# A two-layer decode block on one core: w_o kept by heads, one unit instead of two in small products at a layer's end, and layer 2's rolled block one unit later

## The chip, the cores and the metric

The kernel runs on one core of a Trainium2 chip. The metric is the device time of one execution in microseconds. Three runs of the kernel before took 650.52, 650.72 and 650.79 us; the median is 650.72 us.

A core has five engines with instruction streams of their own: TensorE (PE in the profile; its weight loads are shown apart as PEld), VectorE (DVE), ScalarE (ACT), GpSimd (POOL) and SyncE (SP). SP issues the transfers, and 16 DMA engines carry them out. The engines wait for each other on semaphores. The matmuls write to eight banks of an accumulator memory (`ps`).

## The reference

Four sequences decode one token each, through attention, FFN, attention, FFN, with the same weights twice. Only the shapes matter here:

```python
B, Sq, D = 4, 1, 512
Hq, Hkv, Sk, Dh = 32, 8, 8192, 128
F = 1792
# attention: x + A(layernorm(x))
q = (x @ wq)                       # 32 heads of 128; 4 heads share one key/value head
scores = einsum("bhqd,bhkd->bhqk", q, k) * Dh ** -0.5
o = einsum("bhqk,bhkd->bhqd", softmax(scores), v)
return o.reshape(B, Sq, Hq * Dh) @ wo
# FFN: x + B(layernorm(x))
return (silu(x @ w_gate) * (x @ w_up)) @ w_down
```

All inputs are bf16. The key and value caches have 2 MB for each of the 32 pairs of a sequence and a key/value head. They are read once per layer, except for what the second layer still finds on the chip.

## The kernel before, in words

**Units.** A unit is one pair of a sequence b and a key/value head g, u = 4 g + b. Layer 1 takes the units 0 to 31. Layer 2 starts with 29, 30 and 31, whose K and V are still on the chip (`NRES = 3`), and then takes 0 to 28 (`unit_order`, line 310). Each unit needs 2 MB of K and 2 MB of V. Eight slots of 2 MB hold them; `home` (line 336) says which slot.

**One unit.** K arrives with 64 positions per partition. DVE transposes it in eight pieces (`turn`), PE multiplies each piece with the placed query (`scores`, four products of 256 columns per piece). Then come the softmax steps: the row maximum (`max_p`, `max_t`), the exponent on ACT (`exps`), a transpose of the probabilities on DVE (`turn_p`), and the sum and its reciprocal (`total`). The values are multiplied in `values` (line 551) in one of two ways:

- wide: 16 products whose moving operand has 512 columns of V. The result holds every combination of a position group and a slice of V, of which only a part is wanted. ACT copies the first slice with a factor (`own_first`), DVE adds three more (`own_others`), and a product with `head` sums the rows (`add_rows`). All of this goes through one buffer, `acc`. `scale_o` then writes the scaled result to `oT`.
- small: 64 products of 4 columns with V as the weights (`block_last`). The result is the output itself, and only `scale_o` follows.

`NLAST` (line 181) says how many of a layer's last units take the small way. Their V is worked in eight blocks; a layer's last V is loaded in four parts (`split`), so that its blocks can start before all of it is there.

**Output projection.** After the fourth unit of a head group, `out_proj` (line 631) multiplies `oT` with the 512 rows of w_o that belong to it. w_o lies on the chip with 4 KB per partition and group, that is four consecutive rows of w_o. So the rows in `oT` are first reordered: 16 products with columns of the identity matrix (`pick`), a cast on DVE into `o4`, then 16 products with `wo_sb`, then an addition to `xT`. The cast is what waits for w_o's arrival.

**Order.** Nothing is scheduled at run time. Python lists write the order down: `blocks` holds PE's larger pieces, each with a length in us; `advance` counts these lengths down against two lists of follow-up steps, `line` (the softmax of the next unit) and `after` (the sums and scaling of the one before). `flush` empties them where a buffer is needed again. In `block_last`, `flush(after)` stands before the seventh of eight blocks. The instructions of PE, DVE and ACT are recorded on tapes first. `roll` (line 740) finds, for each layer, a stretch that repeats with period four (`CYCLE`), and writes it as a loop with register arithmetic; what is left before and after it is written out. Each engine's loop has its own start and number of turns.

**Transfers.** SP issues all of them in one order (`items`, `pump`): w_q, x, then K and V in the order of use, with a quarter of w_o after each of the positions 3, 6, 9 and 12. A load goes out when its slot is free. At a layer's end w_gate, w_up and w_down follow into slots 6 and 7 and a strip behind them. When the FFN's products are through, the loads of the next units go there. `runs` (line 345) views the source as at least 32 rows of at most 32 KB, so that one transfer has few and long packets.

**Instruction code.** Engines fetch their instructions by DMA as well; the profile shows them as a queue of their own.

Of the kernel before, what the change touches and what calls it, by code (L numbers as in the profile page):

```python
# [8 lines left out]
BF16 = mybir.dt.bfloat16  # L9
U8 = mybir.dt.uint8  # L10
# [135 lines left out]
def bass_interleave_layers__gqa_block_cached__swiglu_ffn__decode_kernel(  # L146
# [12 lines left out]
    B, _, D = A_x.shape  # L159
    _, G, S, Dh = A_k_cache.shape  # L160
    HqDh = A_wq.shape[1]
    Hq = HqDh // Dh
    F = B_w_gate.shape[1]
    REP = Hq // G
    P = 128
# [3 lines left out]
    XB = KT * B  # L169
# [3 lines left out]
    QB = 32  # L173
# [4 lines left out]
    assert XQ <= SW  # L178
    ZP = QB - REP
    NQ = 4  # L180
    NLAST = 2
    NSLOT = 8
    NKEEP = 6
    NV = NB // 2
    RUN = 1 << 15
# [5 lines left out]
    with ExitStack() as es:  # L191
        sb = lambda name, shape, dt: es.enter_context(nc.sbuf_tensor(name, shape, dt))
# [20 lines left out]
        WD = ((0, 6), (6, 12), (12, 14))  # L213
        wq_sb = sb("wq_sb", [P, KT, HqDh], BF16)

        wo_sb = sb("wo_sb", [P, G, REP, D], BF16)
        wo_b = wo_sb[:].rearrange("p g e n -> p (g e n)").bitcast(U8)
        identf = sb("identf", [P, P], FP32)

        ident = identf[:].bitcast(BF16).rearrange("p (x e) -> p x e", e=2)[:, :, 1]  # L220
# [2 lines left out]
        quad = sb("quad", [P, NA], BF16)  # L223
        head = sb("head", [P, REP], FP32)
        rstd = sb("rstd", [P, B], FP32)
        o4 = sb("o4", [P, REP, B], BF16)
        oT = sb("oT", [P, 2, REP, B], BF16)

        acc = sb("acc", [P, Dh], FP32)
# [5 lines left out]
        pb = sb("pb", [P, SW], BF16)  # L235
# [3 lines left out]
        rl = sb("rl", [P, 4, REP], FP32)  # L239
# [4 lines left out]
        n = 2 * FO * B  # L244
# [7 lines left out]
        def bank(k):  # L252
            return ps[:, k * BANKF:(k + 1) * BANKF]

        def bank_bf(k):
# [4 lines left out]
        STEP, TOT, OUTB, LNB = 4, 5, 6, 7  # L260
# [8 lines left out]
        sem_w = {n: [sem(f"sem_{n}{i}") for i in range(c)]  # L269
                 for n, c in (("wq", KT), ("wo", 4), ("wg", 1), ("wu", 2), ("wd", 3))}  # L270
# [32 lines left out]
        rl_of = {}  # L303
# [38 lines left out]
                return 0 if i == NU - 1 else (7, 2, 3, 6)[i % CYCLE]  # L342
            return {NU - 3: 1, NU - 2: 4, NU - 1: 5}.get(i, (5, 0, 4, 1)[i % CYCLE])

        def runs(src):

            n = src.shape[0] * src.shape[1] * 2
            return src.rearrange("(r k) n -> r (k n)", r=32 * -(-n // (32 * RUN)))

        def load_weight(name, i=0):  # L350
            if name == "wq":
                T.dma("sp", [(wq_sb[:, i, :], runs(A_wq[i * P:(i + 1) * P, :]))], sem_w["wq"][i], writes=[f"wq{i}"])
            elif name == "wo":
                n = G // 4
                w = REP * Dh
                T.dma("sp", [(wo_sb[:, g, :, :].rearrange("p e n -> p (e n)"), runs(A_wo[g * w:(g + 1) * w, :]))
                             for g in range(i * n, (i + 1) * n)], sem_w["wo"][i], writes=[f"wo{i}"])
            elif name == "wg":
                T.dma("sp", [(wg_sb[:, k, :], runs(B_w_gate[k * P:(k + 1) * P, :])) for k in range(KT)], sem_w["wg"][0],
                      writes=places + ["wg"])  # L360
            elif name == "wu":
                up = [(wu_sb[k], runs(B_w_up[k * P:(k + 1) * P, :])) for k in range(KT)]
                if i == 0:
                    T.dma("sp", up[:FR], sem_w["wu"][0], writes=["wu"])
                T.dma("sp", up[FR:], sem_w["wu"][1], writes=["wu3"])
            else:

                for j, (a, b) in enumerate(WD):
                    T.dma("sp", [(wd_sb[:, f:f + 2, :].rearrange("p e n -> p (e n)"),
                                  runs(B_w_down[f * P:(f + 2) * P, :])) for f in range(a, b, 2)], sem_w["wd"][j],  # L370
                          writes=[f"wd{j}"])
# [179 lines left out]
        def values(L, u):  # L551
            g, b = unit_gb(u)
            bk = OBK[turn_of[u]]
            def begin():
                flush(line, u)
                flush(after, turn_of[u])

            def end():
                finished(("V", L, u))
                after.extend(rest)  # L560

            def block(i):

                if i == 0:
                    begin()
                s = slot_of["V", L, u]
                v = kv[:, s, :].rearrange("p (q t d) -> p t q d", t=TB, d=Dh)
                for t in range(TB):
                    j = t % NA
                    c0 = t * QB + i * NV * REP  # L570
                    T.pe(bank(bk)[j * QB:j * QB + NV * REP, :], pT[:, turn_of[u], c0:c0 + NV * REP],
                         v[:, t, NV * i:NV * (i + 1), :],
                         reads=[f"s{s}.{NV * i + k}" for k in range(NV)] + [f"pT{turn_of[u]}"], writes=[f"pb{bk}"],
                         sig=(t == TB - 1), start=(i == 0 and t == j), stop=(i == 1 and t >= TB - NA))
                if i == 1:
                    end()

            def own_first():
                T.op("act", lambda e: e.activation(acc[:], bank(bk)[:, 0:Dh], ACTF.Copy, scale=own[:, 0:1]),
                     reads=[f"pb{bk}", "own"], writes=["acc"])  # L580

            def own_others():
                for k in range(1, NV):
                    T.op("dve", lambda e: e.scalar_tensor_tensor(acc[:], bank(bk)[:, k * Dh:(k + 1) * Dh], own[:, k:k + 1],
                                                                 acc[:], op0=ALU.mult, op1=ALU.add),
                         reads=[f"pb{bk}", "own", "acc"], writes=["acc"])

            def add_rows():
                T.pe(bank(LNB)[:, 0:REP], acc[:], head[:], reads=["acc", "head"], writes=[f"pb{LNB}"],
                     start=True, stop=True)  # L590
                scale_o(LNB)

            def block_last(q):

                if q == 0:
                    begin()
                if q == NB - 2:
                    flush(after)
                s = slot_of["V", L, u]
                for t in range(q * TB, (q + 1) * TB):  # L600
                    c0 = (t % TB) * QB + REP * q
                    T.pe(bank(bk)[:, 0:REP], kv[:, s, t * Dh:(t + 1) * Dh], pT[:, turn_of[u], c0:c0 + REP],
                         reads=[f"s{s}.{q}", f"pT{turn_of[u]}"], writes=[f"pb{bk}"], sig=(t % TB == TB - 1),
                         start=(t == 0), stop=(t == TT - 1))
                if q == NB - 1:
                    end()

            def scale_o(k):
                T.op("dve", lambda e: e.tensor_tensor(oT[:, g // (G - 1), :, b], bank(k)[:, 0:REP], rl[:, rl_of[u], :],
                                                      ALU.mult),  # L610
                     reads=[f"pb{k}", f"rl{rl_of[u]}"], writes=[f"oT{g // (G - 1)}"])

            if u in unit_order[L][-NLAST:]:
                rest = [[0.3, turn_of[u], lambda: scale_o(bk)]]
                blocks.extend((0.25, lambda q=q: block_last(q)) for q in range(NB))
            else:
                rest = [[0.1, None, own_first], [0.6, turn_of[u], own_others], [1.3, None, add_rows]]
                blocks.extend((0.5, lambda i=i: block(i)) for i in range(2))
            done.add((L, u))
            if all((L, g * B + k) in done for k in range(B)):  # L620
                rest.append([0.5, None, lambda: out_proj(g)])


# [4 lines left out]
        def wo_at(n):  # L628
            return lambda g: wo_b[:, bass.ds(g * (REP * D * 2) + n * 2, P * 2)].bitcast(BF16)

        def out_proj(g):

            pick = ident.rearrange("p (j e) -> p e j", e=REP)
            ob = bank(OUTB)[:, XB:2 * XB].rearrange("p (e b) -> p e b", b=B)
            for c in range(REP):
                for h in range(REP):
                    T.pe(ob[h * QB:(h + 1) * QB, c, :], pick[:, c, :], oT[:, g // (G - 1), h, :],
                         reads=[f"oT{g // (G - 1)}", "ident"], writes=[f"pb{OUTB}"], sig=(h == REP - 1),
                         start=True, stop=True)
            T.op("dve", lambda e: e.tensor_copy(o4[:], ob),  # L640
                 reads=[f"pb{OUTB}"] + [f"wo{i}" for i in range(4)], writes=["o4"])
            for nt in range(KT):
                for c in range(REP):
                    T.pe(bank(OUTB)[:, nt * B:(nt + 1) * B], ((c, nt), wo_at(c * D + nt * P)), o4[:, c, :], at=g,
                         reads=["o4"], writes=[f"pb{OUTB}"], sig=(c == REP - 1), start=(c == 0), stop=(c == REP - 1))
            add_to_x()


# [91 lines left out]
        def roll(name):  # L740
# [18 lines left out]
            for L in range(2):  # L759
                run = {}  # L760
                for n in range(L * NU + 1, L * NU + NU - CYCLE - 1):
# [2 lines left out]
                            strides(m) == strides(n + (m - n) % CYCLE):  # L764
                        m += 1
                    run[n] = m - n
                n = max(run, key=run.get)
                turns = run[n] // CYCLE + 1
                assert turns >= 3
                step = {}  # L770
# [87 lines left out]
```

## Time and profile before

| | |
|---|---|
| median of 3 runs | 650.72 us |
| the profiled execution's own time | 651.29 us |
| its span, first to last instruction | 649.3 us |
| PE busy | 505.3 us (78%), 4896 products |
| DVE busy | 446.2 us (69%) |
| ACT busy | 116.3 us (18%) |
| DMA, mean over the span | 422 GB/s, 274.27 MB |
| chain that ended last | DMA 50%, DVE 24%, PE 21% |
| w_o's transfers | 8 of 512 KB, 37.7 us to landing (median) |
| pick products, `ps<-oT,identf` | 256, 6.6 us busy in all |
| w_o products, `ps<-o,wo_sb` | 256, 26.5 us busy in all |
| casts, `o<-ps` | 16, 2.3 us busy in all |
| small value products, `ps<-pT,kvf` | 256, 7.8 us busy in all |

How to read it. "Busy" is the time in which at least one instruction of that engine ran. PE's products are pipelined, so that the sum of their durations is more than the busy time. Almost all instructions stand on two lines of the program, L99 for PE and L117 for DVE and ACT, because two helpers record them; one goes by the names of what is written and read. `kvf` is the memory of the eight slots and the FFN's weights, `pb` and `pT` the probabilities before and after the transpose, `acc` the buffer of the sums, `ps` the accumulator banks, `scr` scratch space. "idle before <- X" names what ended a wait; "issue" stands for time in which the engine waited for no semaphore that the profile shows. In the strips of 40 slices each slice is 16.2 us.

### The profile page before, as it was taken

What the parts mean: (1) busy time and instruction counts of PE and PEld (TensorE: products, weight loads), DVE (VectorE), ACT (ScalarE), POOL (GpSimd) and SP (SyncE); (2) the same over time, 40 slices, a digit from 0 to 9 for tenths busy, and PEclk for the clock granted to TensorE, in tenths of its full rate; (3) what the DMA queues carried; (4) which work ended last, traced back from release to release, by engine and by line L of the source; (5) the groups of instructions that cost most, each with busy time, mean ns of one, the idle gap of its engine ahead of it and who ended that gap; (6) DMA issues with size and microseconds to landing.
All of it is one profiled execution on the core that took longest, in us unless ns stands there. A gap on an engine that the chain in (4) does not pass through costs nothing.

```text
span 649.3 us, 12407 instructions
## 1 busy us (share of the span) xinstructions
PE 505.3 (78%) x4896; PEld 324.7 (50%) x4896; DVE 446.2 (69%) x1079; ACT 116.3 (18%) x391; POOL 19.3 (3%) x73
## 2 busy tenths in 40 slices
PE   1657788878868787886877986898888787886886
PEld 1534454545435454553556654555555454553556
DVE  2556676776866767776762386979797777686683
ACT  0021111211211212221220211213131221121120
POOL 0000000000000000000000000000000000000000
PEclk9998787797987879789795978979897969799795
DMA  8999999999999999999999999999999999999996
GB/s 347 427 431 428 433 429 434 428 440 428 432 436 424 444 426 432 439 424 442 428 416 361 421 408 430 417 439 430 432 438 424 438 430 436 436 424 438 430 415 279
DMA packets 13085, 274.27 MB, mean 422 GB/s; under 512 B 2712, under 2 KB 2720, under 8 KB 3744
## 3 DMA queue, kind: packets, MB, share of 16 engines
q1 hardware_dynamic: 13056, 273.89, 98.7%
q8 instruction: 17, 0.28, 0.2%
q14 instruction: 12, 0.10, 0.0%
HBM read 273.88 MB, written 0.00 MB: 422 GB/s over the span
## 4 chain that ended last, share of the span: by engine, by line
DMA 50%; DVE 24%; PE 21%; issue 3%; SPq 1%; ACT 1%; DVEq 0%; POOL 0%; ACTq 0%; POOLq 0%
DMA kvf<-in_A_k_cache_dram 47%; PE ps L99 21%; DVE kvf L117 15%; DVE acc L117 4%; DMA kvf<-in_B_w_up_dram 3%; DVE one L117 1%; DVE pT L117 1%; SPq L135 1%; DVE m L117 1%; DVE scr L117 1%; ACT pb L117 0%; ACT acc L117 0%; DVE oT L117 0%; DVEq L782 0%; SPq L133 0%
## 5 line engine op out<-in xcount | busy, mean ns | idle before, releaser
L117 DVE STREAM_TRANSPOSE kvf<-kvf 128x512 f32<-128x512 f32 x488 | 322.3, 686 | 68.6 <-DMA kvf<-in_A_k_cache_dram 68.6
L99 PE MATMUL ps<-kvf,zq 128*128 128x256 bf16 x2048 | 332.6, 305 | 21.7 <-DVE kvf L117 16.4
L99 PEld LDWEIGHTS ps<-kvf,zq 128*128 128x128 bf16 x2048 | 202.6, 111 | 92.7 <-DVE kvf L117 40.2
L117 ACT ACTIVATE pb<-m 1x128 f32<-1x128 f32 x64 | 19.7, 308 | 441.1 <-DVE m L117 441.1
L99 PE MATMUL ps<-kvf,pT 128*16 128x512 bf16 x960 | 68.0, 407 | 1.4 <-DVE rl L117 1.4
L117 DVE SCALAR_TENSOR_TENSOR acc<-ps,own,acc 128x128 f32<-128x128 f32 x180 | 63.2, 351 | 6.5 <-ACT acc L117 1.9
L99 PE MATMUL ps<-identf,one 128*1 128x128 f32 x64 | 17.9, 279 | 43.2 <-DVE one L117 43.2
L117 DVE TENSOR_REDUCE one<-ps 128x1 f32<-128x256 f32 x64 | 25.9, 405 | 37.0 <-PE ps L99 36.5
L99 PEld LDWEIGHTS ps<-identf,one 128*1 128x1 f32 x64 | 5.1, 80 | 73.6 <-DVE one L117 67.5
L99 PE MATMUL ps<-head,acc 128*128 128x4 f32 x120 | 24.5, 275 | 21.4 <-DVE acc L117 21.3
L99 PEld LDWEIGHTS ps<-head,acc 128*128 128x128 f32 x120 | 20.5, 214 | 37.0 <-DVE acc L117 36.7
L117 ACT ACTIVATE pb<-ps,one,rstd 128x256 bf16<-128x256 f32 x64 | 36.1, 563 | 2.1
L467 POOL TENSOR_TENSOR zq<-scr,quad 128x64 bf16<-128x64 bf16 x62 | 18.1, 293 | 604.0 <-PE ps L99 564.9
L99 PEld LDWEIGHTS ps<-kvf,pT 128*16 128x16 bf16 x960 | 19.1, 91 | 33.8 <-issue 21.9
L99 PE MATMUL ps<-one,pb 1*128 1x1 f32 x128 | 26.2, 272 | 11.5 <-ACT pb L117 11.2
L99 PEld LDWEIGHTS ps<-one,pb 1*128 1x128 f32 x128 | 20.8, 202 | 28.8 <-ACT pb L117 26.0
L99 PE MATMUL ps<-o,wo_sb 128*128 128x4 bf16 x256 | 26.5, 166 | 9.1 <-DVE o L117 9.1
L117 DVE STREAM_TRANSPOSE pT<-pb 128x256 bf16<-128x256 bf16 x64 | 26.1, 408 | 9.7 <-ACT pb L117 9.7
L99 PEld LDWEIGHTS ps<-rsm,one 128*128 128x128 f32 x128 | 23.9, 232 | 12.2 <-ACT rsm L117 10.4
L99 PEld LDWEIGHTS ps<-o,wo_sb 128*128 (+1 forms) x256 | 22.8, 103 | 12.8 <-issue 9.0
L99 PE MATMUL ps<-rsm,one 128*128 128x4 f32 x128 | 21.7, 240 | 9.0 <-ACT rsm L117 9.0
L117 DVE TENSOR_TENSOR xT<-xT,ps 128x16 f32<-128x16 f32 x21 | 3.6, 172 | 33.1 <-PE ps L99 33.1
(61 smaller groups left out, 197.1 us busy)
## 6 DMA issues: line engine op xcount, KB each, us to landing
kvf<-in_A_k_cache_dram SPq DMA_DIRECT2D x60, 2048.0 KB, 28.8
kvf<-in_A_v_cache_dram SPq DMA_DIRECT2D x58, 2048.0 KB, 31.2
wq_sb<-in_A_wq_dram SPq DMA_DIRECT2D x4, 1024.0 KB, 8.4
wo_sb<-in_A_wo_dram SPq DMA_DIRECT2D x8, 512.0 KB, 37.7
kvf<-in_A_v_cache_dram SPq DMA_DIRECT2D x8, 512.0 KB, 14.7
kvf<-in_B_w_gate_dram SPq DMA_DIRECT2D x8, 448.0 KB, 16.8
kvf<-in_B_w_down_dram SPq DMA_DIRECT2D x14, 256.0 KB, 17.6
kvf<-in_B_w_up_dram SPq DMA_DIRECT2D x5, 448.0 KB, 18.0
```

The source lines that it names most:

```text
L99: return e.matmul(out, lhsT=lhsT if at is None else lhsT(place(at)), rhs=rhs, **kw)
L117: self.tape[engname].append((repr((name, args, kw)), lambda e, _: getattr(e, name)(*args, **kw), left, sig, None))
L135: ins = e.add_instruction(mybir.InstDMACopy(name=self.nc.get_next_instruction_name(), mode="Copy", queue="qSPDynamicHW", ins=e.lower_ap_dm ...
L467: T.op(eng, lambda e: e.tensor_tensor(dst, q4, m4_, ALU.mult), reads=keys_ + ["quad"], writes=["zq"])
```

## The change

- `wo_sb` has one row of 1 KB per partition and head: partition p of head h holds row 128 h + p of w_o. It is loaded with 32 transfers of 128 KB (eight per quarter) instead of eight of 512 KB (two per quarter). Each transfer has 16 source rows of 8 KB.
- `out_proj` takes `oT` as it is. The pick products, the cast and `o4` are gone. The wait for w_o's four quarters stands at `scale_o` of a group's last unit.
- `NLAST` is 1. The unit before a layer's last (30 in layer 1, 27 in layer 2) has its values in 16 wide products, with the sums through `acc`.
- `roll` takes, among the starts with the same number of turns, the last one. In layer 2 PE's and ACT's loops begin a unit later (the 6th unit of the layer in the kernel before, the 7th after); in layer 1 the starts are as they were. The number of turns stays 7 and 6 for PE and ACT, and 6 and 6 for DVE.

```diff
-    NLAST = 2
+    NLAST = 1
...
-        wo_sb = sb("wo_sb", [P, G, REP, D], BF16)
-        wo_b = wo_sb[:].rearrange("p g e n -> p (g e n)").bitcast(U8)
+        wo_sb = sb("wo_sb", [P, Hq, D], BF16)
+        wo_b = wo_sb[:].rearrange("p h n -> p (h n)").bitcast(U8)
...
-        o4 = sb("o4", [P, REP, B], BF16)
...
-        def runs(src):
+        def runs(src, least=32):
 
             n = src.shape[0] * src.shape[1] * 2
-            return src.rearrange("(r k) n -> r (k n)", r=32 * -(-n // (32 * RUN)))
+            return src.rearrange("(r k) n -> r (k n)", r=least * -(-n // (least * RUN)))
...
-                n = G // 4
-                w = REP * Dh
-                T.dma("sp", [(wo_sb[:, g, :, :].rearrange("p e n -> p (e n)"), runs(A_wo[g * w:(g + 1) * w, :]))
-                             for g in range(i * n, (i + 1) * n)], sem_w["wo"][i], writes=[f"wo{i}"])
+                n = Hq // 4
+                T.dma("sp", [(wo_sb[:, h, :], runs(A_wo[h * Dh:(h + 1) * Dh, :], 16)) for h in range(i * n, (i + 1) * n)],
+                      sem_w["wo"][i], writes=[f"wo{i}"])
...
+            done.add((L, u))
+            whole = all((L, g * B + k) in done for k in range(B))
...
-                     reads=[f"pb{k}", f"rl{rl_of[u]}"], writes=[f"oT{g // (G - 1)}"])
+                     reads=[f"pb{k}", f"rl{rl_of[u]}"] + [f"wo{i}" for i in range(4) if whole],
+                     writes=[f"oT{g // (G - 1)}"])
...
-            done.add((L, u))
-            if all((L, g * B + k) in done for k in range(B)):
+            if whole:
                 rest.append([0.5, None, lambda: out_proj(g)])
...
         def out_proj(g):
-
-            pick = ident.rearrange("p (j e) -> p e j", e=REP)
-            ob = bank(OUTB)[:, XB:2 * XB].rearrange("p (e b) -> p e b", b=B)
-            for c in range(REP):
-                for h in range(REP):
-                    T.pe(ob[h * QB:(h + 1) * QB, c, :], pick[:, c, :], oT[:, g // (G - 1), h, :],
-                         reads=[f"oT{g // (G - 1)}", "ident"], writes=[f"pb{OUTB}"], sig=(h == REP - 1),
-                         start=True, stop=True)
-            T.op("dve", lambda e: e.tensor_copy(o4[:], ob),
-                 reads=[f"pb{OUTB}"] + [f"wo{i}" for i in range(4)], writes=["o4"])
+            k = g // (G - 1)
             for nt in range(KT):
                 for c in range(REP):
-                    T.pe(bank(OUTB)[:, nt * B:(nt + 1) * B], ((c, nt), wo_at(c * D + nt * P)), o4[:, c, :], at=g,
-                         reads=["o4"], writes=[f"pb{OUTB}"], sig=(c == REP - 1), start=(c == 0), stop=(c == REP - 1))
+                    T.pe(bank(OUTB)[:, nt * B:(nt + 1) * B], ((c, nt), wo_at(c * D + nt * P)), oT[:, k, c, :], at=g,
+                         reads=[f"oT{k}"], writes=[f"pb{OUTB}"], sig=(c == REP - 1), start=(c == 0), stop=(c == REP - 1))
             add_to_x()
...
-                n = max(run, key=run.get)
+                n = max(run, key=lambda n: (run[n] // CYCLE, n))
```

## The prediction

> **What bounds the kernel now.** I read the page's slices first, then busy time by stretch, then the chain of waits around the layers' ends, then the order of time in the last 20 us.
>
> ```profile
> DMA  8999999999999999999999999999999999999996
> GB/s 347 427 431 428 433 429 434 428 440 428 432 436 424 444 426 432 439 424 442 428 416 361 421 408 430 417 439 430 432 438 424 438 430 436 436 424 438 430 415 279
> ...
> q8 instruction: 17, 0.28, 0.2%
> ```
>
> ```profile
> core 0: us, PE busy (x) PEld busy (x) DVE busy (x) ACT busy (x) POOL busy (x), PEclk, DMA share, GB/s
> 80.00:300.00 220.00, 177.13 (x1431) 109.35 (x1431) 158.47 (x371) 39.45 (x134) 6.73 (x23) 0.84 1.00 433
> ...
> 27.00:68.00 41.00, 28.00 (x269) 18.18 (x267) 26.83 (x60) 6.83 (x23) 1.17 (x4) 0.84 1.00 427
> ...
> 344.00:346.00 2.00, 1.26 (x48) 1.29 (x49) 1.14 (x5) 0.25 (x1) 0.00 (x0) 0.50 1.02 414
> 346.00:349.00 3.00, 1.32 (x44) 1.15 (x41) 0.21 (x1) 0.00 (x0) 0.00 (x0) 0.50 0.49 197
> ...
> 386.00:510.00 124.00, 103.68 (x912) 64.23 (x911) 102.73 (x242) 26.00 (x88) 4.39 (x15) 0.92 1.00 430
> ```
>
> The DMA engines are full from 2 to 346 us and again to 643 us: 274 MB at 433 GB/s. No compute in those stretches costs anything. Time can be won or lost in three ways: more DMA time per byte; the hole at 346-349 us, where 197 GB/s instead of 433 means (433 - 197)/433 x 3 = 1.6 us without data; and the tail, once the last weights are there.
>
> The hole, by the chain of waits:
>
> ```profile
> 326.13 18.47 DMA kvf<-in_B_w_up_dram
> 344.61 0.14 issue
> 344.74 1.50 PE ps L99 x51
> 346.24 1.38 issue
> 347.62 0.31 PE ps L99 x5
> 347.92 0.02 issue
> ```
>
> w_up lands at 344.6, PE does 51 of the 56 up products, stands 1.38 us for "issue" (no semaphore, no data), does the last 5, and at 347.99 SP issues the next K, because slot 6 holds w_gate and w_up until then.
>
> The tail, PE in order of time:
>
> ```profile
> 644.10 1.27 PE L99 MATMUL ps<-scr,kvf 128*128 128x4 bf16 x35 [0.43 <-DVE scr L117]
> 645.69 0.70 PE L99 MATMUL ps<-scr,kvf 128*128 128x4 bf16 x21 [0.32 <-issue]
> 646.72 0.59 PE L99 MATMUL ps<-identf,xn 128*4 128x128 bf16 x4 [0.33 <-DVE xn L117]
> ```
>
> From 631 us on the end hangs on a serial chain of small operations (attention, w_o, layer norm, FFN), with another 0.32 us of "issue".
>
> **The change, part by part.**
>
> *w_o on the DMA engines.* 4.19 MB come in 32 transfers of sixteen 8 KB source rows, each spread as eight pieces of 1 KB, instead of 8 transfers of thirty-two 16 KB rows with four pieces of 4 KB. The trace's record of single packets gives 615 ns (median) for w_o's 16 KB packets, 309 ns for 8 KB of a half K or V (one piece), 314.5 ns for w_down's 8 KB (four pieces of 2 KB): 1.8 ns for a further piece. Eight pieces: 309 + 7 x 1.8 = 322 ns. Per engine 32 x 322 = 10.3 us against 16 x 615 = 9.84 us; 24 more semaphore packets of 9 ns add 0.2 us. I take +0.7 us. Lower end 0, since the packet time may not grow with pieces at all. Upper end: each piece as long as a whole 1 KB packet of x (48.5 ns), 32 x (8 x 48.5 - 309) ns = +2.5, with the semaphores about +2.6 us. w_down is the nearest row (several pieces in a packet, queue full), hence 0.7. It is paid in full: DMA is the bound there.
>
> [...]
>
> *w_o on SP.* 24 more issues of 0.60 us (8 now, median 0.599) are 14.4 us of SP, before K2, K3, K4, K5 and their V. Cover: w_o's transfers land 24 to 44.7 us after issue. At 1.35 us each, which w_down's seven took (9.42 us) behind a full queue, it is 32 us; K5 would still be issued at about 60 us, ahead of the last w_o landing (issued 27.7, landed by 72.4). Cost 0; if that cover were gone, the DMA would idle for the difference.
>
> *The wait for w_o* moves from the cast on DVE to the scaling of unit 3, 1.0 us earlier (312.03 and 313.02 in a later group). Transposes queue behind it, and PE's scores behind those. The first w_o product ran at 80.1 us, w_o was there at 72.4 at the latest. Cost 0.
>
> *Pick products and casts* (256 of PE, about 0.41 us per group; 16 of DVE, 0.14 us) go. In 14 of 16 groups the DMA share is 1.00: worth 0. At a layer's end they are on the chain and in the sums below.
>
> *Layer 1's end.* By the changed order, PE does units 29 and 30 wide, unit 31's softmax products, 48 of 31's 64 small products, then add_rows(29) and add_rows(30) side by side, then the last 16, then w_o. There is one acc, so unit 30's copy (ACT) and its three sums (DVE) can start only after add_rows(29). On before's clock: exp of 31 ends at 335.5; DVE's transpose follows at 335.6, not 336.12, since the scaling of 29 no longer stands ahead of it; 0.45 transpose and 0.36 sum product put the 48 at 336.4; they take 1.3 (40 took 1.21 in the tail) to 337.7; add_rows 0.39, copy 0.34, sums 1.12, add_rows(30) and the last 16 together 0.78, scaling 0.17, w_o 0.59, handoffs of 0.05 each: x is added at 341.4 instead of 340.31. That is +1.1 us, although pick and cast (1.0 us with their handoffs) are out of it. With w_o's 0.7 the gate products, which ended at 343.76, end at 345.6. w_up lands at 345.3. So the up products start at 345.6 instead of 344.74.
>
> *The 1.38 us.* PE fetched 17 blocks of 16 KB, 256 instructions of 64 B; the trace has fetches at 337.1 and 345.1, and the stall ends 2.5 us after the second began. Counting the built program (two instructions a bf16 product, four an fp32 one), a block border lies at the 52nd up product, and the one before at the first w_o product (an idle of 0.57 there, 0.28 at the same place in the tail). Ahead of the FFN the changed program is 156 instructions shorter (32 in the loop, 32 pick, 92 in unit 30), so the borders move 78 products on: one to the second up product, the next into layer 2's q projection. From entering a block to having the next took 7.9 us (339.7 to 347.6) and 4.9 (tail). The changed PE enters the block before the up products at about 337.4, so that one is there by 342.3 to 345.3, before 345.6. The stall goes; what is late next is the gate chain, not w_up. Bounds: 0 and -1.4; I take -1.4.
>
> [...]
>
> *Sum at the hole.* Up products end at 345.6 + 1.5 = 347.1 instead of 347.92: SP's K goes out 0.8 us earlier. The DMA's old work ends 0.7 later. 1.6 us of hole shrink to 0.1, and everything after is 0.7 - 1.5 = -0.8 us. Layer 2's compute starts at w_down's products, also 0.8 earlier, so the short lack of loads near 384 us stays as it is.
>
> *Layer 2's block.* One more unit unrolled before PE's and ACT's loop. ACT waits 5.4 us for "issue" at 393-398 us, where the loop begins; from 386 on the DMA share is 1.00, which hides it. Bounds: 0, as nothing on a hidden path can gain, and +5.4 us if it fell where the queue of loads is short (384 us). I take 0, since a unit later lies further into the full stretch.
>
> *The tail.* Units 27 and 28 in the same order as 30 and 31, with a w_o step for group 6 between. Same rows, same count: 48 small products end at 635.25, then add_rows, copy, sums, add_rows, scaling to 637.85, w_o 0.59, the last 16 (0.45), scaling, w_o, x added at 639.85 instead of 638.73: +1.1. The border of the stall moves out of w_down: 1.65 us for 56 products (as at 348.22) instead of 2.29, -0.6. PE is at half clock from 635 us (fp32 products 0.59 us at 639.17 against 0.39 at 632.97); the two add_rows now fall there: +0.3. Together +0.8. Nothing of it waits for DMA: w_down's last part landed at 645.5.
>
> *Total*: -0.8 + 0.8 = 0.0 on a span of 649.3 us. The profiled execution took 651.29 us, 0.57 over the median of 650.72; on the median it is **650.7 us**.
>
> **Rivals.**
>
> *A, slower: a code block comes late after all.* Entered at 345.6, the next block needs 4.9 to 7.9 us, 350.5 to 353.5; PE needs it at about 351 in the q projection. At the long end PE stands 2.5 us, and layer 2's first loads, which wait on compute (364-384 us), go out as much later: 653.2. It decides from a fetch above 5.4 us. Against it: the DMA has its hole then, and the fetch begun at 349.1 found free engines. 0.19.
>
> *B, slower: 1 KB pieces cost 2.6 us.* Then w_up lands at 347.2, the up products end at 348.7, the hole's end is 0.8 later than before, not earlier: 650.7 + 1.6 = 652.3. For it: 414 against 433 GB/s at 2 KB already. 0.11.
>
> *C, slower: a fixed cost per transfer on the rings.* [...] By rows: if the 0.6 us that SP takes to issue one were also the time of the engines for one, 32 x 0.6 = 19.2 against 9.9 us, and behind the hole's slack of 1.6 some 8 us would remain: 659. [...] 414 GB/s at 256 KB speaks against it. 0.02.
>
> *D, faster: PE's clock.* PE ran at half clock from 338 to 359 us, and layer 2's first 28 score products took 5.45 us there (195 ns each, 125 when the clock is full: 3.5). With less small work before and an earlier start, the full clock may come a step earlier, 1.4 us won where layer 2's loads wait on compute: 649.3. Half clock in every such stretch before speaks against it. 0.18.
>
> **How the numbers follow.** Two runs of this kernel can be told apart from about 0.2%, 1.3 us. Forecast 0.50 (its own range 649.6 to 651.9: w_o's 0 to 1.4, the tail's +-0.5), D 0.18, A 0.19, B 0.11, C 0.02. So faster 0.18, same 0.50, slower 0.32. The range 649.0 to 653.3 holds the forecast, D, B and most of A.
>
> **What would show it.** w_o: the rate in 27-68 us (427 now) a little lower, and K28 landing earlier by 0.8. Hole: the "issue" of 1.38 gone, the up products started by PE's own work, 346-349 us above 300 GB/s. Tail: two fp32 add_rows with 1.5 us of ACT and DVE between them on the chain, no "issue" in w_down's products. Wrong if an "issue" shows in layer 2's q projection, if w_up ends the wait for the up products, or if the rate falls below 400 where w_o is loaded.

## The result, and the profile after

The changed kernel takes 660.24 us (median; 658.25 to 660.3), the kernel before in the same series 650.62 us. The ratio is 1.0142, with a 95% interval of 1.0122 to 1.0163: slower by 1.4%, outside the predicted range of 649.0 to 653.3 us. The profiled execution of the changed kernel took 658.25 us with a span of 656.5 us, 7.1 us more than the span before. It was the fastest of the four, the other three took 660.2 to 660.3 us; so the trace below accounts for 7.1 of the 9.6 us between the medians, and what the slower executions lost in addition is not shown.

The slices of the changed kernel's page (DMA share and GB/s), and its line of issues for w_o:

```profile
DMA  8999999999999999999999999999999999999996
GB/s 366 408 372 366 356 433 430 430 439 431 431 431 433 435 429 433 434 429 433 439 414 386 383 428 429 431 430 433 431 437 429 433 429 437 429 433 433 433 415 271
...
wo_sb<-in_A_wo_dram SPq DMA_DIRECT2D x32, 128.0 KB, 21.9
```

The second to fifth slices, 16 to 82 us, carry 356 to 408 GB/s where the kernel before had 427 to 433. These are the slices in which w_o is loaded. The later full slices are as before, apart from those around the border of the layers. In the second to fifth slice the DMA share is a 9, that is 90% or more, so the engines are not idle: they are busy for longer with the same bytes. Busy time by stretch in the changed kernel (columns as before: PE, PEld, DVE, ACT, POOL, granted clock, DMA share, GB/s):

```profile
27.00:68.00 41.00, 24.42 (x215) 14.82 (x212) 21.54 (x48) 5.06 (x17) 1.17 (x4) 0.79 1.01 373
```

373 GB/s at a DMA share of 1.01, against 427 at 1.00. The prediction had named a rate below 400 here as the sign that it was wrong.

The rest of the change came about nearly as forecast. The hole at layer 1's end, PE in order of time in the changed kernel:

```profile
351.33 0.89 PE L99 MATMUL ps<-xn,kvf 128*128 128x4 bf16 x28
353.15 1.64 PE L99 MATMUL ps<-xn,kvf 128*128 128x4 bf16 x56 [0.94 <-DMA kvf<-in_B_w_up_dram]
355.10 0.80 PE L99 MATMUL ps<-scr,kvf 128*128 128x4 bf16 x24 [0.31 <-DVE scr L117]
356.82 1.01 PE L99 MATMUL ps<-scr,kvf 128*128 128x4 bf16 x32 [0.93 <-DMA kvf<-in_B_w_down_dram]
```

The 56 up products now run in one piece; the 1.38 us of "issue" after the 51st are gone. And the tail:

```profile
641.31 0.38 PE L99 MATMUL ps<-head,acc 128*128 128x4 f32 x2
643.32 0.59 PE L99 MATMUL ps<-head,acc 128*128 128x4 f32 x2 [1.62 <-DVE acc L117]
...
651.86 1.65 PE L99 MATMUL ps<-scr,kvf 128*128 128x4 bf16 x56 [0.83 <-DVE scr L117]
```

Two sums of rows with 1.62 us of waiting for `acc` between them, and 56 down products without "issue", both as forecast.

The loss can be dated from the single packets in the trace: 60 MB had landed at 143.7 us before and at 151.3 us after (+7.5); 140 MB at +7.5; 200 MB, behind the hole, at +6.9, and 260 MB at +7.0. So w_o costs 7.5 us, the hole gives back some 0.6, and the end adds 0.1 to 0.2: 7.1 us, the difference of the spans. Two profiles of kernels that load w_o equally fast differ by up to 0.8 us in such a landing time, so the small terms are rough. The packets themselves: w_o's 512 packets of 8 KB took 438 ns in the median (5 to 95%: 319 to 589), not the 322 ns of the forecast, and K's and V's packets beside them, 1214 ns elsewhere, were stretched too (1307.5 ns in the median of those that began between 27 and 68 us). The term for w_o on the DMA engines is the one to be explained.

### The profile page after: what moved, and what is told of

Same layout as the page of the kernel before. It is cut to its first block, busy times and chain, and to the rows that moved or that the text cites. A ratio compares the mean times of both kernels' runs of the same rounds, so it can differ in the third digit from the quotient of the medians.

```text
span 656.5 us, 11727 instructions
## 1 busy us (share of the span) xinstructions
PE 507.1 (77%) x4548; PEld 322.2 (49%) x4548; DVE 448.4 (68%) x1069; ACT 117.1 (18%) x393; POOL 19.2 (3%) x73
## 4 chain that ended last, share of the span: by engine, by line
DMA 53%; PE 20%; DVE 18%; issue 4%; SPq 3%; ACT 1%; DVEq 0%; ACTq 0%; POOL 0%; POOLq 0%
DMA kvf<-in_A_k_cache_dram 51%; PE ps L99 20%; DVE kvf L117 11%; DVE acc L117 3%; SPq L135 3%; DMA kvf<-in_B_w_down_dram 2%; DVE one L117 1%; DVE pT L117 1%; DVE m L117 1%; ACT pb L117 0%; DVE scr L117 0%; ACT acc L117 0%; DVE oT L117 0%; SPq L133 0%; DVEq L774 0%
## 5 line engine op out<-in xcount | busy, mean ns | idle before, releaser
L99 PE MATMUL ps<-kvf,zq 128*128 128x256 bf16 x2048 | 336.6, 309 | 21.7 <-DVE kvf L117 12.3
L99 PEld LDWEIGHTS ps<-kvf,zq 128*128 128x128 bf16 x2048 | 205.9, 112 | 92.4 <-DVE kvf L117 36.6
L99 PE MATMUL ps<-kvf,pT 128*16 128x512 bf16 x992 | 74.0, 425 | 2.1 <-DVE rl L117 2.1
L117 DVE SCALAR_TENSOR_TENSOR acc<-ps,own,acc 128x128 f32<-128x128 f32 x186 | 65.3, 351 | 7.2 <-ACT acc L117 2.3
L99 PE MATMUL ps<-head,acc 128*128 128x4 f32 x124 | 26.4, 283 | 20.9 <-DVE acc L117 20.9
L99 PEld LDWEIGHTS ps<-head,acc 128*128 128x128 f32 x124 | 22.9, 230 | 36.5 <-DVE acc L117 35.9
L99 PEld LDWEIGHTS ps<-rsm,one 128*128 128x128 f32 x128 | 23.5, 228 | 15.0 <-ACT rsm L117 13.3
L99 PE MATMUL ps<-oT,wo_sb 128*128 128x4 bf16 x256 | 26.5, 166 | 5.2 <-DVE oT L117 5.2
L99 PEld LDWEIGHTS ps<-oT,wo_sb 128*128 (+1 forms) x256 | 22.1, 100 | 12.3 <-issue 8.2
L117 ACT ACTIVATE one<-ps,rstd 128x1 f32<-128x1 f32 x64 | 16.7, 261 | 39.8 <-PE ps L99 26.5
```

The costliest lines, as they stand in the source:

```text
L99: return e.matmul(out, lhsT=lhsT if at is None else lhsT(place(at)), rhs=rhs, **kw)
L117: self.tape[engname].append((repr((name, args, kw)), lambda e, _: getattr(e, name)(*args, **kw), left, sig, None))
```

## The experiments

**What made w_o slow: first series.** The changed kernel differs in three respects at once: pieces of 1 KB, 32 transfers instead of 8, and 16 source rows, each spread over eight partitions. Theory 1, a supposition at this point: the eight partitions cost; a packet that reaches that far meets another engine's packets where both write. The rivals: the small pieces, and a fixed cost per transfer. Four kernels take these apart. Before took 650.5 us in this series.

*w32*: the changed kernel, the same 32 transfers and the same 1 KB pieces, seen as 32 rows of 4 KB (four partitions per packet).

```diff
-                T.dma("sp", [(wo_sb[:, h, :], runs(A_wo[h * Dh:(h + 1) * Dh, :], 16)) for h in range(i * n, (i + 1) * n)],
+                T.dma("sp", [(wo_sb[:, h, :], runs(A_wo[h * Dh:(h + 1) * Dh, :])) for h in range(i * n, (i + 1) * n)],
```

> The changed kernel, but each of w_o's 32 transfers is viewed as 32 source rows of 4 KB (4 partitions each) instead of 16 rows of 8 KB (8 partitions each). Pieces stay 1 KB, transfers stay 32. Theory 1 (a packet that spreads over 8 partitions makes DMA engines meet at the same part of the memory): the packets take 155 to 165 ns for 4 KB, the rate in 27-68 us returns from 373 to about 425 GB/s, the time falls by about 8 to 9 us, to 650 to 652. Theory 2 (1 KB pieces are slow by themselves): the mean packet is half of the 445 ns of now, about 220 ns, the rate stays near 373, the time 658 to 660. Theory 3 (32 transfers of 128 KB cost a fixed time each on the DMA engines): 658 to 660 as well. [...]

Measured: 651.6 us, ratio to before 1.0016 (1.0002 to 1.003). Its stretch:

```profile
27.00:68.00 41.00, 28.60 (x302) 18.97 (x299) 26.13 (x59) 6.84 (x23) 1.17 (x4) 0.83 1.00 420
```

420 GB/s, and 1024 packets of 4 KB at 164 ns, 10.46 us per engine in sum, against 9.88 in the kernel before and 14.25 in the changed one. One argument takes back 8.6 of the 9.6 us. The 1 KB pieces, the 32 transfers and all the rest of the change together cost about 1 us, at most 2 by the interval.

*w128*: the same with 128 rows of 1 KB, one partition per packet.

```diff
-                T.dma("sp", [(wo_sb[:, h, :], runs(A_wo[h * Dh:(h + 1) * Dh, :], 16)) for h in range(i * n, (i + 1) * n)],
+                T.dma("sp", [(wo_sb[:, h, :], A_wo[h * Dh:(h + 1) * Dh, :]) for h in range(i * n, (i + 1) * n)],
```

> The changed kernel, but each of w_o's transfers is viewed as 128 source rows of 1 KB, so that packet and piece are the same and each packet goes to one partition. Theory 1 (8 partitions in a packet): packets of 45 to 50 ns, as x's (46 to 48.5), per engine 32 x 8 x 48 = 12.3 us against 9.9 in the kernel before: 653 to 654, between w32 and the changed kernel. Theory 2 (1 KB pieces slow by themselves, 55 ns each): 658 to 660. Theory 3 (number of transfers): 658 to 660.

Measured: 652.56 us, 1.0026 (1.0014 to 1.0038), a little less than theory 1 had expected. 1 KB packets at 46 ns add up to 11.84 us per engine. Even the smallest packets cost less than the 8 KB ones of the change.

*b16*: the kernel before, its eight transfers of 512 KB seen as 16 rows of 32 KB (eight partitions per packet, pieces of 4 KB).

```diff
-                T.dma("sp", [(wo_sb[:, g, :, :].rearrange("p e n -> p (e n)"), runs(A_wo[g * w:(g + 1) * w, :]))
+                T.dma("sp", [(wo_sb[:, g, :, :].rearrange("p e n -> p (e n)"), A_wo[g * w:(g + 1) * w, :].rearrange("(r k) n -> r (k n)", r=16))
```

> The kernel before, but w_o's 8 transfers are viewed as 16 source rows of 32 KB (8 partitions each) instead of 32 rows of 16 KB (4 partitions each). Pieces stay 4 KB, transfers stay 8. Theory 1 (8 partitions in a packet): slower by 4 to 9 us, 655 to 660, packets of w_o well above 1214 ns for 32 KB. Theories 2 (1 KB pieces) and 3 (number of transfers): no change, 650 to 651, packets of 1214 ns.

Measured: 664.29 us, 1.0207 (1.0175 to 1.0238), more than expected.

```profile
27.00:68.00 41.00, 23.26 (x220) 15.01 (x216) 20.32 (x45) 5.06 (x17) 1.17 (x4) 0.75 1.01 338
```

The largest packets and the fewest transfers of all give 338 GB/s, worse than the change itself. In the first lot of w_o its 32 KB packets take some 2110 ns (28 to 30 us); K's and V's of the same size take 1214 elsewhere. So neither small pieces nor many transfers are needed.

*w32_two*: w32 with two units in small products, as before.

```diff
-    NLAST = 1
+    NLAST = 2
```

> As w32 (32 source rows), and NLAST back to 2: the last two units of a layer in small products. Against w32 this undoes only the wide way of the second-last unit. My sum for that part: the tail's chain gets shorter by about 1.1 us (no second copy, three sums and add_rows on the chain) plus 0.3 of half clock; the code blocks of PE move on by 92 instructions in each layer, so an 'issue' of up to 1.4 us may come back at the hole or in the tail. Theory 'chain': 1 to 1.5 us faster than w32. Theory 'code blocks decide': equal or slower than w32, with an 'issue' of over 0.3 us at a layer's end.

Measured: 650.59 us, 0.9995 (0.9985 to 1.0005). Against w32 the second unit in small products is worth 1.0 us, within the 1 to 1.5 expected from the chain through one `acc`. All that is left of the change in this kernel (w_o's new place in 32 transfers, no picks and casts, the later loop) is worth nothing that can be measured against before.

**Second series.** All slow kernels so far have two things in common: eight partitions per packet, and 16 packets in a transfer, one for each of the 16 engines if they are dealt out evenly (the trace doesn't name a packet's engine; in the kernel before, the 32 packets of w_o's first transfer begin as 16 between 27.63 and 28.36 us and 16 more, each 0.61 us after one of the first). The next two kernels take these apart, from the kernel before (650.73 us here).

*b_half*: each 512 KB transfer in two of 64 partitions, 16 rows of 16 KB each. The packets are those of the kernel before, four partitions each, but one per engine and transfer.

```diff
-                T.dma("sp", [(wo_sb[:, g, :, :].rearrange("p e n -> p (e n)"), runs(A_wo[g * w:(g + 1) * w, :]))
-                             for g in range(i * n, (i + 1) * n)], sem_w["wo"][i], writes=[f"wo{i}"])
+                T.dma("sp", [(wo_sb[s * 64:(s + 1) * 64, g, :, :].rearrange("p e n -> p (e n)"),
+                              A_wo[g * w + s * 256:g * w + (s + 1) * 256, :].rearrange("(r k) n -> r (k n)", r=16))
+                             for g in range(i * n, (i + 1) * n) for s in range(2)], sem_w["wo"][i], writes=[f"wo{i}"])
```

> The kernel before, with each 512 KB transfer of w_o split into two of 64 partitions (16 of 256 KB; 16 source rows of 16 KB each). A packet still fills four partitions with 4 KB each, and every engine gets the same packets in the same order, but one per transfer instead of two. Theory 1 (what costs is a packet that reaches over eight partitions): as before, 650.5 us +-1, packets of 16 KB at 612 to 616 ns (median). Rival (what costs is that a transfer has only one packet per engine, as in the changed kernel and in the kernel with rows of 32 KB): 655 to 664 us, packets of 16 KB clearly above 700 ns.

Measured: 659.72 us, 1.0131 (1.0106 to 1.0157), packets at 1062 ns (before: 614). That is what the rival had foretold.

```profile
27.00:68.00 41.00, 24.21 (x240) 15.01 (x236) 20.39 (x46) 5.07 (x17) 1.17 (x4) 0.77 1.01 358
```

Theory 1 in its first form falls: four partitions per packet can be as slow as eight.

*b64*: the kernel before with 64 rows of 8 KB, two partitions per packet.

```diff
-                T.dma("sp", [(wo_sb[:, g, :, :].rearrange("p e n -> p (e n)"), runs(A_wo[g * w:(g + 1) * w, :]))
+                T.dma("sp", [(wo_sb[:, g, :, :].rearrange("p e n -> p (e n)"), A_wo[g * w:(g + 1) * w, :].rearrange("(r k) n -> r (k n)", r=64))
```

> The kernel before, with w_o's eight transfers seen as 64 source rows of 8 KB, two partitions of 4 KB per packet. Theory 1, with packets that reach over two partitions instead of four: as before, 650.5 us +-1, 512 packets of 8 KB at 309 ns, the size that took 438 ns (median) in the changed kernel. Rival (8 KB is a size of packet that goes badly between K and V's 32 KB): packets around 438 ns and 655 to 660 us.

Measured: 650.76 us, 1.0005 (0.9995 to 1.0015), 512 packets of 8 KB at 309 ns. The same number of packets of the same size as in the changed kernel, with nothing lost.

*w32_first*: w32 with layer 2's loop where it was before.

```diff
-                n = max(run, key=lambda n: (run[n] // CYCLE, n))
+                n = max(run, key=run.get)
```

> The kernel with w_o in rows of 4 KB (651.6 us), with layer 2's loop beginning at its 6th unit, as in the kernel before. My theory: the loop's place is hidden behind full transfers; 651.6 us +-0.8, an idle ACT of some 5.4 us for issue is back at 390 to 400 us, DMA share 1.00 there. Rival: the later loop costs what the trace of w32 does not show as a wait; then 650.5 us or less.

Measured: 652.51 us, 1.0029 (1.0017 to 1.0042). The median is 0.9 us over w32, which ran in another series, and the intervals against before overlap. The idle time of 5.4 us on ACT, which I had tied to the loop's place, did not come back; PE waited instead:

```profile
395.35 1.66 PE L99 MATMUL ps<-kvf,zq 128*128 128x256 bf16 x8 [3.94 <-issue]
```

ACT's own line of the changed kernel shows that its wait had only moved a unit on with the loop:

```profile
412.99 0.26 ACT L117 ACTIVATE one<-ps,rstd 128x1 f32<-128x1 f32 x1 [6.02 <-issue]
```

So I read the wait as one for code that is being fetched, which falls elsewhere when the code in front differs: a block of 8 KB was fetched at 396.6 us in the kernel before, within ACT's wait (393.0 to 398.4), and three at 410.5 to 410.9 us in the changed kernel, within its wait (407.0 to 413.0). No run tests this alone. Both places cost little, as forecast.

*b_one*: the kernel before with one unit in small products and nothing else changed.

```diff
-    NLAST = 2
+    NLAST = 1
```

> The kernel before, with one unit instead of two in small products at a layer's end, and nothing else changed. By the chain of operations at a layer's end (two sums of rows through one acc): +1 us at each end, of which the hole at 347 us takes one only in part: 651.5 to 652.5 us. The code is 92 instructions shorter ahead of the FFN, so that the border of the code blocks moves by 46 products, from the 52nd up product to about the 42nd down product: the idle time for issue leaves the up products. Rival: the saved idle pays for the longer chain, 650.5 us +-0.4.

Measured: 652.4 us, 1.0022 (1.0011 to 1.0033). The longer chain costs 1.4 us (0.7 to 2.1), although the "issue" has left the up products here as well:

```profile
343.13 2.43 PE L99 MATMUL ps<-xn,kvf 128*128 128x4 bf16 x84
345.94 0.80 PE L99 MATMUL ps<-scr,kvf 128*128 128x4 bf16 x24 [0.38 <-DVE scr L117]
347.60 0.88 PE L99 MATMUL ps<-scr,kvf 128*128 128x4 bf16 x24 [0.86 <-DMA kvf<-in_B_w_down_dram]
```

**Third series: one packet per transfer, or where the engines write?** What was left: the rival "one packet per engine and transfer", and theory 1 in a new form: what counts is which partitions a transfer covers, since packets meet where they write. Which partitions go badly together no run so far shows, apart from 0-63 and 64-127. Two kernels take the place and the number of packets apart. If the place counts, two packets per engine and transfer don't help partitions 0-63 and 64-127: by b_half, half of 1062 ns, 531, for a packet of half the size, and 659.7 us again. And 64 partitions elsewhere, 32-95, can reach the 614 ns of the kernel before with one packet per engine and transfer. By the rival it is the other way round. Both start from the kernel before (650.22 us here).

*b_half2*: as b_half, with 32 rows of 8 KB: two packets per engine and transfer, still 64 partitions. Against b_half:

```diff
-                              A_wo[g * w + s * 256:g * w + (s + 1) * 256, :].rearrange("(r k) n -> r (k n)", r=16))
+                              A_wo[g * w + s * 256:g * w + (s + 1) * 256, :].rearrange("(r k) n -> r (k n)", r=32))
```

> The kernel before, w_o in 16 transfers of 64 partitions as in the last series, but each seen as 32 source rows of 8 KB (two partitions of 4 KB per packet), so that every engine has two packets per transfer. Rival (one packet per engine and transfer is what costs): as before, 650.7 us +-1, packets of 8 KB at 309 ns. [...]

Measured: 666.75 us, 1.0242 (1.0222 to 1.0262), packets of 8 KB at 551 ns (b64: 309). The packets are as theory 1 would have them (551 against 531 ns), the time is 7 us above b_half's. Per engine w_o's packets add up to 17.40 us against 16.16 in b_half; why the whole loses so much more than b_half is open.

```profile
27.00:68.00 41.00, 24.98 (x232) 15.44 (x228) 20.39 (x45) 5.06 (x17) 1.17 (x4) 0.76 1.02 339
```

*b_mid*: one packet per engine and transfer throughout, but first partitions 32 to 95 (16 rows of 16 KB), and then 0 to 31 and 96 to 127 (16 rows of 8 KB each).

```diff
-                T.dma("sp", [(wo_sb[:, g, :, :].rearrange("p e n -> p (e n)"), runs(A_wo[g * w:(g + 1) * w, :]))
-                             for g in range(i * n, (i + 1) * n)], sem_w["wo"][i], writes=[f"wo{i}"])
+                T.dma("sp", [(wo_sb[lo:hi, g, :, :].rearrange("p e n -> p (e n)"),
+                              A_wo[g * w + lo * 4:g * w + hi * 4, :].rearrange("(r k) n -> r (k n)", r=16))
+                             for part in (((32, 96),), ((0, 32), (96, 128)))
+                             for g in range(i * n, (i + 1) * n) for lo, hi in part], sem_w["wo"][i], writes=[f"wo{i}"])
```

> The kernel before, w_o's 512 KB transfers split into three, all with 16 source rows, one packet per engine: partitions 32 to 95 (rows of 16 KB, four partitions per packet), 0 to 31 and 96 to 127 (rows of 8 KB, two partitions). Rival (one packet per engine and transfer): all of them slow, the 16 KB packets near the 1062 ns that they had with partitions 0 to 63 and 64 to 127; 658 us or more. [...]

Measured: 657.61 us, 1.0107 (1.0091 to 1.0124), just under the 658 us of the rival, so that the time alone does not decide.

```profile
27.00:68.00 41.00, 24.25 (x203) 14.48 (x199) 21.80 (x48) 5.07 (x17) 1.17 (x4) 0.79 1.01 374
```

The packets decide (w_o's, from the trace's record of single packets, ns):

| kernel | rows of a transfer, partitions | packets | median | 5 to 95% |
|---|---|---|---|---|
| before | 32, 0-127 | 256 of 16 KB | 614 | 611-616 |
| b_half | 16, 0-63 and 64-127 | 256 of 16 KB | 1062 | 720-1107 |
| b_mid | 16, 32-95 | 128 of 16 KB | 615 | 611-1212 |
| b_mid | 16, 0-31 and 96-127 | 256 of 8 KB | 515 | 309-631 |
| b64 | 64, 0-127 | 512 of 8 KB | 309 | 309-311 |
| b_half2 | 32, 0-63 and 64-127 | 512 of 8 KB | 551 | 309-725 |
| after | 16, 0-127 | 512 of 8 KB | 438 | 319-589 |

b_half and b_mid have the same 16 KB rows, 64 partitions and one packet per engine. With partitions 0-63 and 64-127 a packet takes 1062 ns, with 32-95 it takes 615. So it is not the single packet per transfer but the place. In b_mid's first lot 31 of the 32 such packets took 611 ns; the last, which began 0.45 us after the first packet of the outer parts, took 1286. In the last two lots the last quarter of them took some 1185 ns (median), when the outer parts had begun as well. The rival falls: the place counts, as theory 1 in its new form has it. That packets meet there is not shown.

How far the runs carry it: that the place of the partitions decides, by 64 partitions that begin at 0 or 64 or at 32, is shown (1062 and 615 ns). One thing moves along with the place: the rows of w_o that are read lie 128 KB further on in b_mid's inner part. A cause on the side of the source would have to depend on that, at the same row length and the same distance between rows; no run moves the source alone. Why one place is slower than another, and whether two packets meet there, is not shown. For the changed kernel this means: that its 16 rows are the cause is shown by w32; that its packets meet is my supposition.

## Why the prediction was wrong, and where it was right

**The step that failed is "w_o on the DMA engines"**: 0.7 us, bounds 0 to +2.6, measured +7.5 in the trace (8.6 between the medians of the changed kernel and w32). It took the price of a packet from its size and number of pieces, and w_down's 8 KB packets (314.5 ns) as the nearest row. On its own ground that was right: w32 has the 1 KB pieces and the 32 transfers, and by the same landing time it loses 0.4 us. But every packet of a weight or a cache in the trace of before comes from a transfer with at least 32 source rows. The change is the first with 16, as its diff says (`least=32` becoming 16 for w_o), and the price of that cannot be read off any of those rows. The upper end, each piece priced as a 1 KB packet of its own, was no bound: it is worked out from packets of x at 48.5 ns, and w_o's packets of one size took 614 ns in the kernel before and 1062 ns in b_half, with rows and pieces of the same size. w128, which really has 1 KB packets throughout, came out at 652.56 us, next to the 652.3 of rival B; its w_o packets cost 2.0 us per engine more than before, within that bound.

**Rival B** had the right place and sign with the wrong cause. **Rival C** (659 us) had nearly the time, and the wrong cause as well: w32 has the same 32 transfers and 651.6 us, so that the 32 transfers and the rest of the change together cost it about 1 us against before. What speaks against a fixed cost in the trace of before are w_down's transfers of 256 KB, behind w_up's at 344 to 346 us, where the rate is 414 GB/s.

**w_o on SP**: the cost of 0 is right, the price was low. The four lots of eight issues took 5.1, 18.3, 13.3 and 14.2 us, 50.9 in all, against 5.0 for the eight before: 45.9 us more, where the forecast had 32 at most. But the next K went out at 60.6 us, as forecast, and the DMA share stayed near 1.0. **The wait for w_o** cost nothing, as forecast: no engine shows a wait that ends with one of its transfers.

**The 1.38 us of issue**: right that it goes; it is gone in the changed kernel and in w32, w128 and w32_first, and so is the 0.32 in the tail. The count of blocks holds against the trace of before: from the first w_o product at 339.69 us, behind 0.57 us of idle time, to the idle time behind the 51st up product PE's stream has 256 instructions (127 weight loads, 127 products, 2 on semaphores), and each of the 17 blocks has 16,384 B, 64 B for an instruction. But the 1.38 us were no fixed price of the kernel before. b64 gives PE the same instructions as the kernel before, and its 56 up products run with at most 0.3 us between them:

```profile
344.78 1.94 PE L99 MATMUL ps<-xn,kvf 128*128 128x4 bf16 x56 [2.30 <-DMA kvf<-in_B_w_up_dram]
```

The other kernels with these instructions show 1.01 (b_half), 1.28 (b16), 0.74 (b_mid) and none (b_half2) at this place. b64 takes 650.76 us all the same, so that the 1.4 us that the forecast took off for it rest on one trace. "What is late next" was wrong: the forecast was the gate chain, and w_up still ended the wait (0.94 us above), since the gate chain was not as late as computed: unit 31's 48 small products ended at 336.9 us in w32, not at 337.7 plus w_o's delay. In w32, with w_o near its full rate, w_up ends the wait as well:

```profile
345.22 1.63 PE L99 MATMUL ps<-xn,kvf 128*128 128x4 bf16 x56 [0.97 <-DMA kvf<-in_B_w_up_dram]
```

There the up products end at 346.85; the forecast was 347.1.

**The sum at the hole**: forecast -1.5 beside w_o's cost, measured about -0.6 in the changed kernel. In w32 it is -1.3 at 200 MB (from +0.4 at 140 MB to -0.9) and -1.0 at 260 MB, as near to the forecast as such landing times can tell. What is won at the hole itself is lost again where layer 2 begins, and comes back only later. Of w32:

```profile
346.00:348.00 2.00, 1.65 (x56) 1.48 (x53) 0.22 (x2) 0.00 (x0) 0.00 (x0) 0.50 0.82 332
348.00:350.00 2.00, 1.01 (x32) 0.93 (x32) 0.34 (x2) 0.00 (x0) 0.00 (x0) 0.50 1.11 311
350.00:352.00 2.00, 1.18 (x18) 1.01 (x18) 0.95 (x6) 0.00 (x0) 0.00 (x0) 0.50 1.14 492
...
356.00:380.00 24.00, 21.93 (x279) 16.02 (x278) 10.48 (x29) 5.06 (x17) 0.88 (x3) 0.86 1.00 403
```

And of the kernel before:

```profile
346.00:348.00 2.00, 0.54 (x15) 0.36 (x11) 0.05 (x1) 0.00 (x0) 0.00 (x0) 0.50 0.69 275
348.00:350.00 2.00, 1.65 (x56) 1.57 (x56) 0.53 (x4) 0.00 (x0) 0.00 (x0) 0.50 1.14 274
350.00:352.00 2.00, 1.18 (x18) 1.01 (x18) 0.96 (x7) 0.00 (x0) 0.00 (x0) 0.50 0.66 279
...
356.00:380.00 24.00, 21.68 (x276) 15.66 (x275) 9.87 (x27) 5.07 (x17) 0.88 (x3) 0.86 1.02 434
```

The hole does fill, from about 275 to 311-492 GB/s. But in 356-380 us the rate falls from 434 to 403: (434 - 403) x 24 is 0.74 MB, or 1.7 us of transfer. In w32 a part of that is caught up later: the lack of loads that the kernel before has at 380-386 us (363 GB/s) is not there (415), and at 260 MB w32 stands 0.6 us ahead of before. In b_one, which had gained 1.7 us at the hole, nothing is left of it by 158 MB. What holds the loads back there was not tested.

**Layer 1's end and the tail**: right in kind, two sums of rows through one `acc`. Their price, both ends together and less what the hole takes up, is 1.0 us between w32 and w32_two and 1.4 us in b_one (0.7 to 2.1); the forecast's +1.1, of which the hole takes a part, and +0.8 are of that size. **Layer 2's block**: forecast 0; taking it back (w32_first) makes 0.9 us more, at the edge of what the runs can tell apart. **Rival A** did not occur: no "issue" above 0.31 us stands on PE in the changed kernel from layer 1's FFN to 400 us. **Rival D** occurred in part. Layer 2's first 28 score products, before, after and in b64:

```profile
354.04 5.45 PE L99 MATMUL ps<-kvf,zq 128*128 128x256 bf16 x28
362.02 4.70 PE L99 MATMUL ps<-kvf,zq 128*128 128x256 bf16 x28
353.77 4.34 PE L99 MATMUL ps<-kvf,zq 128*128 128x256 bf16 x28
```

The granted clock is 0.50 ahead of them (352-354 us before, 360-362 us after) and 1.00 behind them (359.5-362 us before, 366.7-369 us after). After the change they take 0.75 us less, so the full clock came that much earlier among them (the mean is 0.58 in 354-359.5 us before and 0.68 in 362-366.7 us after). But b64, with PE's instructions as before, takes still less, and w32_two and b_one take 5.51: the change isn't shown to be the cause, nor that the time gains by it.

So the changed kernel, with w_o's rows as in w32, comes close to the forecast: 651.6 us against 650.7. Since one term of the sum, the 1.4 us of "issue", is not the same in every trace of the same instructions, part of this closeness is luck. The 8.6 us on top are one argument of one call. No version was clearly faster than before; w32_two equals it.

## What to carry to other kernels

In this case a transfer's rate depended on which partitions it covered and how its rows lay over them, not only on packet size and number: when a change touches how many rows a source is viewed as, or which partitions a transfer covers, look for a row of the trace with that very shape before taking a price from one that merely has the same packet size. Here 32 or more rows over 128 partitions ran at or near full rate with packets from 4 to 32 KB (420 to 432 GB/s where w_o is loaded), and 16 rows over 128 partitions (338 and 373), or 16 and 32 rows over partitions 0-63 and 64-127 (358 and 339), did not. A DMA share of 1.01 stood here beside 338 GB/s as well as beside 431, so it does not say how fast bytes move: read the GB/s beside it, and the time of single packets.

## What the runs showed of the hardware that was not expected

- A packet in the wrong place took nearly twice its time: 16,384 B in 1102 ns (the middle half of b_half's packets in the first lot) are 14.9 GB/s, against 16,384 B in 611 ns, 26.8 GB/s, in the first lot of the kernel before. If two packets share the time, as theory 1 supposes, the two together have 29.7 GB/s; no run shows that they do.
- The transfers beside them suffer as well: of K's and V's packets of 32 KB that began between 27 and 68 us, one in twenty took more than 1808 ns in the changed kernel and more than 2067 in b_half2 (before: 1214), though their own shape had not changed.
- Gathering more into each packet made it worse: 32 KB packets over eight partitions (b16, +13.8 us) cost more than 8 KB packets over eight partitions (+9.6 us for the whole change). Their pieces are 4 KB instead of 1 KB, and no run tells the size of the packet from the size of the piece.
